# Weight conversion in a PSUM bank, wider spacing and a later pair of subtractions, in a fused attention and two-MLP kernel

## Chip, cores and metric

One core of one Trainium2 chip runs the whole program. The metric is device time in microseconds (us), the median over runs. The engines are PE (TensorE: matmuls, and PEld its weight loads), DVE (VectorE), ACT (ScalarE), POOL (GpSimd) and SP (SyncE, which here issues nearly all DMAs).

## What is computed

The reference, cut to what matters:

```
q, k: RMS-normalised per head (batch 4, 12 heads, 448 tokens, 64 wide), times gains
attn = softmax(q k^T / 8) ; x = attn @ v            # x: 1792 tokens x 768
h = x @ w_in (768x2048) ; g = h * sigmoid(h) ; x = g @ w_out (2048x768)
h = x @ w2_in (768x1024) ; s = h * softmax(h) ; n = layernorm(s) * g_ln
out = n @ w2_out (1024x768)
```

The eight input arrays are float64 in memory. The program itself turns the weights to fp32 while it runs: it reads each number as two 32-bit words and puts an fp32 together from them.

## The kernel before

**Stages.** Attention takes the first 250 us or so. Then comes the first MLP. Its 2048 hidden columns are cut into 8 groups g of 256, its tokens into 4 blocks b of 512, 512, 512 and 256. A step (g, b) has two halves: `mlp1_a` multiplies the tokens by the group's part of `w_in` into two PSUM banks `hp` (pool `ps_mm`, 2 banks; 18 matmuls each, since every operand is a high part and a low remainder, and three products of them are summed), and `mlp1_b` multiplies the result `gt` by `w_out` in six groups of six matmuls, d = 0 to 5, each into a bank `xps`. PE does `mlp1_a` of step i+1 ahead of `mlp1_b` of step i. The steps stand in the order (0,0), (0,1), ... (5,3), then (6,0), (6,1), (7,0), (7,1), (6,2), (7,2), (6,3), (7,3). The last stage is the second MLP. It works on pairs of 128-token tiles as 2x2 blocks, and needs only seven block products where eight would be usual, at the price of sums and differences of blocks.

**PSUM.** There are eight banks. In the first MLP two are `hp`, two belong to `P_["x"]` and four to `P_["y"]`. The six groups of a step take them in the order x y y x y y, so with four y banks each bank comes back one whole step later.

**Who empties them.** ACT reads `hp` twice (`gf`, L872, and `gt`, L873); POOL forms the low part of `gt` (L874). DVE adds every `xps` to its accumulator in SBUF (L897; L895 copies in the first group).

**Conversions.** `stages` is one conversion of 384 columns, by six steps: `load` (SP, a 384 KB DMA into `raw`), `mag` (ACT, L157, absolute value of the high words into `cva`), then on DVE `clamp` (L160), `shift` (L164), `sign` (L168) and `low` (L172), whose result is `cvt`. Then ACT rounds it (`hi`, L127) and POOL takes the remainder (`lo`, L130). From group 1 on the results go either straight to a `slab` in SBUF, or through the staging tile `stg` to DRAM (the `park` tensors, L133), from where `unpark` (L771) brings them back as slabs of 768 KB per half when they are due. For `w2_in` and `w2_out` differences of blocks (`sub`, L192) and a gain (L182) are added. The pools give two `raw`, two `cva`, four `cvt` and four `stg` buffers, so load k waits until `low` of conversion k-2 has read its `raw`.

**Order.** All queues are in the order in which the program emits. A clock in units near a microsecond advances with each group of matmuls (`MM`: 0.2105 for each 512-column matmul, 0.111 for each 256-column one), and `tick` emits each step of a conversion when its time in `STEP[ph]` after the conversion's start has come (load 0, mag 4.5, clamp 5.7, shift 6.3, sign 6.9, low 7.5). Starts of conversions are at least `EV` units apart. Each `xps` addition is emitted with its matmuls, ahead of the conversion steps that come due during them. The second MLP has a planner of its own (`timetable`) that orders by due times; `operands` gives it the chain of sums (`mix`), roundings (`hi`, ACT, L1007) and remainders (`lo`).

Of the kernel before, what the change touches and what calls it, by code (L numbers as in the profile page):

```python
# [11 lines left out]
F32 = mybir.dt.float32  # L12
F32R = mybir.dt.float32r
U32 = mybir.dt.uint32
AF = mybir.ActivationFunctionType
ALU = mybir.AluOpType
AX = mybir.AxisListType
PSUM = bass.MemoryType.PSUM
# [19 lines left out]
HW_MIN = float(np.array(0x38100000, np.uint32).view(np.float32))  # L38
HW_MAX = float(np.array(0x47EFFFFF, np.uint32).view(np.float32))
# [60 lines left out]
def fused_kernel(ctx: ExitStack, tc, nat, qt, gqk, w_in, w_out, w2_in, w2_out, g_ln, out):  # L100
    nc = tc.nc
# [7 lines left out]
    P_ = {}  # L109
# [5 lines left out]
    CB = {}  # L115
# [20 lines left out]
    def stages(src, c, ph, w, g=None, quad=None):  # L136

        n = 384
        k = {}

        def load():
            k["raw"] = P_["cv"].tile([128, n, 2], U32, name="raw", tag="raw", bufs=CB.get("raw"))
            nc.sync.dma_start(out=k["raw"][:, :, :].rearrange("p n t -> p (n t)"),
                              in_=src.bitcast(U32)[:, 2 * c * n:2 * (c + 1) * n])  # L150

        def mag():
            k["lw"], k["hw"] = k["raw"][:, :, 0], k["raw"][:, :, 1]
            a = k["a"] = P_["cv"].tile([128, n], U32, name="cva", tag="cva", bufs=CB.get("cva"))[:, :]
            t = k["t"] = a if ph == 0 else P_["cv"].tile([128, n], U32, name="cvt", tag="cvt", bufs=CB.get("cvt"))[:, :]
            k["af"], k["tf"] = a.bitcast(F32), t.bitcast(F32)
            nc.scalar.activation(out=k["af"], in_=k["hw"].bitcast(F32), func=AF.Abs)  # L157

        def clamp():
            nc.vector.tensor_scalar(out=k["af"], in0=k["af"], scalar1=HW_MIN, scalar2=HW_MAX,  # L160
                                    op0=ALU.max, op1=ALU.min)

        def shift():
            nc.vector.tensor_scalar(out=k["a"], in0=k["a"], scalar1=3, scalar2=0x3FFFFFFF,  # L164
                                    op0=ALU.logical_shift_left, op1=ALU.bitwise_and)

        def sign():
            nc.vector.scalar_tensor_tensor(out=k["t"], in0=k["hw"], scalar=0xC0000000, in1=k["a"],  # L168
                                           op0=ALU.bitwise_and, op1=ALU.bitwise_or)

        def low():
            nc.vector.scalar_tensor_tensor(out=k["t"], in0=k["lw"], scalar=29, in1=k["t"],  # L172
                                           op0=ALU.logical_shift_right, op1=ALU.bitwise_or)
        base = list(zip(STEP[ph], (load, mag, clamp, shift, sign, low)))
        if quad is None:
            return base + list(zip(STEP[ph][6:], halves(lambda: k["tf"], w, CL[ph])))

        name, q = quad

        def gain():  # L180
            if g is not None:
                nc.scalar.activation(out=k["tf"], in_=k["tf"], func=AF.Identity, scale=g)  # L182
            q[name] = k["tf"]

        def sub(o, a, b):

            def f():
                if o == "T1":
                    q[o] = P_["cv"].tile([128, n], F32, name="cvt", tag="cvt", bufs=CB.get("cvt"))[:, :]
                else:  # L190
                    q[o] = q[{"T2": "T1", "T3": "12", "T4": "T2"}[o]]
                nc.vector.tensor_tensor(out=q[o], in0=q[a], in1=q[b], op=ALU.subtract)  # L192
            return f

        def out(x, t):
            return list(zip((t, t + .9, t + 2.9), halves(lambda: q[x], w[x], "p")))
        base.append((8.7, gain))
        if name == "11":
            base += out("11", 9.9)
        elif name == "12":  # L200
            base += [(9.5, sub("T1", "12", "11"))] + out("T1", 10.5)
        elif name == "22":
            base += [(9.5, sub("T3", "22", "12"))] + out("22", 9.3) + out("T3", 11.0) + \
                [(12.0, sub("T2", "22", "T1"))] + out("T2", 12.8)
        else:
            base += out("21", 10.4) + [(11.3, sub("T4", "21", "T2"))] + out("T4", 12.2)
        return base
# [607 lines left out]
    psy = ExitStack()  # L815

    def after_attention():

        late.close()
        P_["x"] = psx.enter_context(tc.tile_pool(name="ps_x", bufs=2, space=PSUM, side="right", reuse_waits="tile"))  # L820
        acc1 = ctx.enter_context(tc.tile_pool(name="acc1", bufs=1))
        x2.append(acc1.tile([128, 2, KD, 256], F32, name="x2_0"))
        acc2 = mlp1.enter_context(tc.tile_pool(name="acc2", bufs=1, reuse_waits="tile"))
        x2.extend([acc2.tile([128, KD, CW[b]], F32, name=f"x2_{b}") for b in range(1, NC)])
        P_["big2"] = mlp1.enter_context(tc.tile_pool(name="big2", bufs=2, reuse_waits="tile"))
        P_["y"] = psy.enter_context(tc.tile_pool(name="ps_y", bufs=4, space=PSUM, reuse_waits="tile"))

    HL = [(0, 1), (1, 0), (0, 0)]

# [15 lines left out]
    def fetch(g, every=6.8):  # L845
        pool = P_["big2"] if g % 2 else big
        enqueue(pool, ws[g], w_in[g], every)
        enqueue(pool, ws[g], w_out[g], every)
# [134 lines left out]
    def op(k, e, took, f, after=(), tiles=(), lat=.15):  # L983
        plan2[k] = [e, took, lat, list(after), list(tiles), None]
        run2[k] = f

    def tens(e, o, a, b, f):
        e.tensor_tensor(out=o, in0=a, in1=b, op=f)  # L988

    def operands(l, p, tile, first, e):  # L990

        r, w = raws[l].setdefault(p, {}), (3, 4)[l]

        def mix(n, e=e):
            def f():
                o, a, b = MIX[l][n]
                if n == "S1":
                    r[n] = raws[l]["S1"]
                tens(en[e], r[o], r[a], r[b], ALU.add if n == "S1" else ALU.subtract)
                r[n] = r[o]  # L1000
            return f

        def hi(n):
            def f():
                k = slots[l].pop(0)
                t = parts[l, p, n] = (k, home[l](k))
                nc.scalar.copy(out=t[1][:, 0], in_=r[n])  # L1007
            return f

        def lo(n):  # L1010
            def f():
                t = parts[l, p, n][1]
                tens((nc.gpsimd, nc.vector)[l], t[:, 1], r[n], t[:, 0].bitcast(F32), ALU.subtract)
            return f
        TM = (1.0 if l == 0 else 1.3) if e == "p" else (.5, .69)[l]
        S1 = ("m%d" % l, p)
        E = {"p": "POOL", "v": "DVE"}[e]

        def key(x, n):
            return (x, l, p, n)  # L1020
        op(key("mix", "S1"), E, TM, mix("S1"), first["21"] + first["22"], [S1] + tile("21") + tile("22"))
        op(key("mix", "S2"), *((E, TM) if l == 0 else ("DVE", .75)), mix("S2", "v" if l else e), first["11"] + [key("mix", "S1"), key("lo", "S1")], [S1] + tile("11"))
        op(key("mix", "S3"), E, TM, mix("S3"), first["11"] + [key("mix", "S1")] + [key("lo", "S1")] * l,
           tile("11") + tile("21"))
        op(key("mix", "S4"), E, TM, mix("S4"), [key("mix", "S2"), key("lo", "12")] + first["12"], [S1] + tile("12"))
        prev = [("hi", l, p - 1, ORDER[l][-1])] if p else []
        for n in ORDER[l]:
            src = {"S1": [S1], "S2": [S1], "S3": tile("21"), "S4": tile("12")}.get(n) or tile(n)
            aft = first[n] if n in first else [key("mix", n)]
            if (l, p, n) == (1, 0, "S1"):  # L1030
                aft = aft + [("add", 0, 1, i) for i in (1, 2, 5)]
            op(key("hi", n), "ACT", (.47, .6)[l], hi(n), aft + prev, src + [("r%d" % l, p, n)])
            op(key("lo", n), ("POOL", "DVE")[l], (1.0, .69)[l], lo(n), [key("hi", n)], src + [("r%d" % l, p, n)])
            prev = [key("hi", n)]
# [192 lines left out]

    steps = [(g, b) for g in range(NMG - 2) for b in range(NC)]
    steps += [(6, 0), (6, 1), (7, 0), (7, 1), (6, 2), (7, 2), (6, 3), (7, 3)]
    EV = 3.7  # L1230

    def spare(x):
        if x < 2:
            enqueue(None, [], parked[x], EV, park=parks[x])
        elif x < 6:
            enqueue4(w2_in, EV, park2[0], x - 2, None)
        else:
            enqueue4(w2_out, EV, park2[1], x - 6, gln4)

    def ahead(g):  # L1240
        if g < NMG - 2:
            fetch(g + 1, EV)
        for x in ((0, ), (1, 2), (3, ), (4, 5), (6, ), (7, 8), (9, ))[g]:
# [143 lines left out]
```

## Time and profile before

| | |
|---|---|
| median of 3 runs | 958.27 us (956.87 to 961.7) |
| the profiled execution | 959.88 us, of which the span from first to last instruction is 958.1 us |
| PE busy | 937.7 us, 98% |
| DVE, POOL, ACT busy | 766.2, 540.1 and 514.6 us |

The page gives busy time by engine, slices of the span, the chain that ended last and the costliest groups of instructions. The trace behind it answers with the instructions of one line or one engine in a stretch, with what ended the idle time before each. "L866 <-ACT gt L873" reads: the instruction of line 866 had to wait, and what ended its wait was the ACT instruction of line 873.

### The profile page before, as it was taken

How to read it: one execution, taken by the hardware profiler on the slowest of the kernel's cores; microseconds unless marked ns; L12 is line 12 of the kernel's file. 1: busy time of each engine (PE TensorE's matmuls, PEld its weight loads, DVE VectorE, ACT ScalarE, POOL GpSimd, SP SyncE). 2: the span in 40 equal slices, each digit the busy share in tenths (PEclk: the TensorE clock that was granted, in tenths of full speed). 3: DMA queues.
4: the chain of work that ended last, by engine and by line, in shares of the span. 5: the costliest groups of instructions: out<-in, count | busy, mean ns of one | idle time of the engine just before them, and what ended most of it. 6: DMA issues, size and time to landing. Idle time of an engine off the chain costs nothing. (4 is left out here: it accounts for less than half of the span.)

```text
span 958.1 us, 15217 instructions
## 1 busy us (share of the span) xinstructions
PE 937.7 (98%) x4981; PEld 774.1 (81%) x4981; DVE 766.2 (80%) x1450; ACT 514.6 (54%) x1215; POOL 540.1 (56%) x679
## 2 busy tenths in 40 slices
PE   8999999999999999999999999899999999999998
PEld 7776676776778888888888888778889889889997
DVE  6999999999648879899889999866223878887885
ACT  6898999999733333344334453443022445455553
POOL 7888889898534354554646455445142445557530
PEclk9999999999999999999999999999999999999999
DMA  6776767775413444555456464686378611111101
GB/s 195 197 222 166 208 193 201 197 201 139 127 34 100 128 121 135 187 157 155 156 165 218 131 184 119 206 299 235 140 301 340 254 34 50 58 59 39 60 1 66
DMA packets 73502, 147.89 MB, mean 154 GB/s; under 512 B 10256, under 2 KB 48912, under 8 KB 73168
## 3 DMA queue, kind: packets, MB, share of 16 engines
q1 hardware_dynamic: 73136, 146.93, 49.4%
q8 instruction: 39, 0.64, 0.3%
q14 instruction: 39, 0.32, 0.1%
q10 hardware_dynamic: 288, 0.01, 0.0%
HBM read 90.44 MB, written 34.60 MB: 131 GB/s over the span
## 5 line engine op out<-in xcount | busy, mean ns | idle before, releaser
L866 PE MATMUL hp<-xt,slab 128*128 128x512 f32 (+1 forms) x1152 | 241.5, 367 | 5.8 <-ACT gt L873 5.8
L889 PE MATMUL xps<-gt,slab 128*128 128x512 f32 (+1 forms) x1152 | 235.6, 363 | 0.0
L866 PEld LDWEIGHTS hp<-xt,slab 128*128 128x128 f32 x1152 | 198.6, 190 | 42.1 <-ACT gt L873 7.3
L889 PEld LDWEIGHTS xps<-gt,slab 128*128 128x128 f32 x1152 | 197.1, 189 | 33.8
L874 POOL TENSOR_TENSOR gt<-gf,gt 128x512 fp32r<-128x512 f32 (+1 forms) x64 | 80.9, 1264 | 117.0 <-ACT gt L873 91.9
L897 DVE TENSOR_TENSOR x<-xps,x 128x512 f32<-128x512 f32 (+1 forms) x168 | 101.4, 615 | 50.8 <-PE xps L889 50.8
L157 ACT ACTIVATE cva<-raw 128x384 f32<-128x384 f32 x96 | 53.5, 560 | 149.3 <-DMA raw<-w_out 78.0
L484 DVE TENSOR_SCALAR_CACHE_REDUCE sp<-sp,ms 128x448 f32<-128x448 f32 x168 | 109.3, 684 | 9.3 <-PE sp L476 7.8
L130 POOL TENSOR_TENSOR stg<-cvt,stg 128x384 fp32r<-128x384 f32 x64 | 72.3, 1136 | 69.3 <-ACT stg L127 69.3
L520 POOL TENSOR_SCALAR p<-p,st 128x448 f32<-128x448 f32 x144 | 97.9, 691 | 18.9 <-DVE st L511 14.0
L495 ACT ACTIVATE p<-sp,st 128x448 f32<-128x448 f32 x144 | 96.7, 686 | 7.8 <-DVE sp L484 7.4
L1056 PE MATMUL y<-slab,gt 128*128 128x384 f32 x504 | 91.7, 341 | 2.3 <-DVE gt L988 2.3
L1056 PE MATMUL x<-slab,xr 128*128 128x512 f32 x378 | 91.9, 395 | 0.0
L1056 PEld LDWEIGHTS y<-slab,gt 128*128 128x128 f32 x504 | 88.6, 191 | 3.3 <-DVE gt L988 2.6
L130 POOL TENSOR_TENSOR slab<-cvt,slab 128x384 fp32r<-128x384 f32 x48 | 54.5, 1137 | 61.3 <-ACT slab L127 61.3
L1056 PEld LDWEIGHTS x<-slab,xr 128*128 128x128 f32 x378 | 69.5, 188 | 14.0 <-ACT gt L1067 0.2
L528 PE MATMUL tp<-ident,p 128*128 128x128 f32 x504 | 77.5, 274 | 1.1 <-ACT ht L557 0.9
L168 DVE SCALAR_TENSOR_TENSOR cvt<-raw,cva 128x384 uint32<-128x384 uint32 x88 | 73.3, 833 | 5.5
L172 DVE SCALAR_TENSOR_TENSOR cvt<-raw,cvt 128x384 uint32<-128x384 uint32 x88 | 72.3, 821 | 2.3
L160 DVE TENSOR_SCALAR cva<-cva 128x384 f32<-128x384 f32 x96 | 43.9, 458 | 34.0 <-ACT cva L157 33.9
L528 PEld LDWEIGHTS tp<-ident,p 128*128 128x128 f32 x504 | 60.8, 140 | 11.3 <-ACT ht L557 2.7
L476 PE MATMUL sp<-Z 128*128 128x448 f32 x138 | 64.3, 466 | 2.5 <-ACT y L318 1.4
(163 smaller groups left out, 1605.5 us busy)
## 6 DMA issues: line engine op xcount, KB each, us to landing
Z<-X SPq DMA_DIRECT2D x92, 224.0 KB, 3.6
raw<-w_in SPq DMA_DIRECT2D x48, 384.0 KB, 3.4
raw<-w_out SPq DMA_DIRECT2D x48, 384.0 KB, 3.2
park<-stg SPq DMA_DIRECT2D x32, 384.0 KB, 4.1
slab<-park SPq DMA_DIRECT2D x16, 768.0 KB, 8.9
nat<-nat SPq DMA_DIRECT2D x23, 480.0 KB, 4.1
vn<-nat SPq DMA_DIRECT2D x24, 256.0 KB, 3.9
park0T<-stg SPq DMA_DIRECT2D x16, 384.0 KB, 4.2
```

The lines of the kernel that those rows point to most:

```text
L130: en[e].tensor_tensor(out=k["o"][1], in0=f(), in1=k["o"][0].bitcast(F32), op=ALU.subtract)
L168: nc.vector.scalar_tensor_tensor(out=k["t"], in0=k["hw"], scalar=0xC0000000, in1=k["a"], op0=ALU.bitwise_and, op1=ALU.bitwise_or)
L172: nc.vector.scalar_tensor_tensor(out=k["t"], in0=k["lw"], scalar=29, in1=k["t"], op0=ALU.logical_shift_right, op1=ALU.bitwise_or)
L484: nc.vector.tensor_scalar(out=sp, in0=sp, scalar1=c["ms"][:, g:g + 1], scalar2=None, op0=ALU.mult, op1=ALU.min, accum_out=c["st"][:, 0, i: ...
L495: nc.scalar.activation(out=P(i), in_=c["sp"][i][:, :], func=AF.Exp, bias=c["st"][:, 0, i:i + 1], scale=-1.0, accum_out=c["st"][:, 1, i:i + 1])
L520: nc.gpsimd.tensor_scalar(out=p, in0=p, scalar1=r, scalar2=0.0, op0=ALU.mult, op1=ALU.add)
L528: nc.tensor.transpose(tp[:, o + t * 128:o + (t + 1) * 128], p[:, a:a + 128], ident[:, :])
L866: nc.tensor.matmul(hp[0][:, 0:CW[b]], ws[g][0][:, pw, kd * 256 + m * 128:kd * 256 + (m + 1) * 128], xT[(b, kd)][:, px, :], start=(i == 0), ...
L874: nc.gpsimd.tensor_tensor(out=gt[0][:, 1, m, :], in0=gf[:, :], in1=gt[0][:, 0, m, :].bitcast(F32), op=ALU.subtract)
L889: nc.tensor.matmul(xps[:, 0:CW[b]], ws[g][1][:, pw, m * 768 + d * 128:m * 768 + (d + 1) * 128], gt[0][:, px, m, :], start=(j == 0), stop=( ...
L897: nc.vector.tensor_tensor(out=o, in0=xp, in1=o, op=ALU.add)
L1056: nc.tensor.matmul(ps(b), s_[:, px, k, :], W[l, PAIR[x]][:, pw, k * n:(k + 1) * n], start=(not k0 and j == 0), stop=(j == 3 * w - 1), skip ...
```

## The change

```diff
         def mag():
             k["lw"], k["hw"] = k["raw"][:, :, 0], k["raw"][:, :, 1]
-            a = k["a"] = P_["cv"].tile([128, n], U32, name="cva", tag="cva", bufs=CB.get("cva"))[:, :]
-            t = k["t"] = a if ph == 0 else P_["cv"].tile([128, n], U32, name="cvt", tag="cvt", bufs=CB.get("cvt"))[:, :]
-            k["af"], k["tf"] = a.bitcast(F32), t.bitcast(F32)
-            nc.scalar.activation(out=k["af"], in_=k["hw"].bitcast(F32), func=AF.Abs)
+            k["a"] = P_["cv"].tile([128, n], U32, name="cva", tag="cva", bufs=CB.get("cva"))[:, :]
+            nc.scalar.activation(out=k["a"].bitcast(F32), in_=k["hw"].bitcast(F32), func=AF.Abs)
 
         def clamp():
-            nc.vector.tensor_scalar(out=k["af"], in0=k["af"], scalar1=HW_MIN, scalar2=HW_MAX,
+            k["p"] = k["a"] if ph == 0 else P_["cp"].tile([128, 512], U32, name="cp", tag="cp")[:, 0:n]
+            nc.vector.tensor_scalar(out=k["p"].bitcast(F32), in0=k["a"].bitcast(F32), scalar1=HW_MIN, scalar2=HW_MAX,
                                     op0=ALU.max, op1=ALU.min)
 
         def shift():
-            nc.vector.tensor_scalar(out=k["a"], in0=k["a"], scalar1=3, scalar2=0x3FFFFFFF,
+            nc.vector.tensor_scalar(out=k["p"], in0=k["p"], scalar1=3, scalar2=0x3FFFFFFF,
                                     op0=ALU.logical_shift_left, op1=ALU.bitwise_and)
 
         def sign():
-            nc.vector.scalar_tensor_tensor(out=k["t"], in0=k["hw"], scalar=0xC0000000, in1=k["a"],
+            nc.vector.scalar_tensor_tensor(out=k["p"], in0=k["hw"], scalar=0xC0000000, in1=k["p"],
                                            op0=ALU.bitwise_and, op1=ALU.bitwise_or)
 
         def low():
-            nc.vector.scalar_tensor_tensor(out=k["t"], in0=k["lw"], scalar=29, in1=k["t"],
+            t = k["a"] if ph == 0 else P_["cv"].tile([128, n], U32, name="cvt", tag="cvt", bufs=CB.get("cvt"))[:, :]
+            k["tf"] = t.bitcast(F32)
+            nc.vector.scalar_tensor_tensor(out=t, in0=k["lw"], scalar=29, in1=k["p"],
                                            op0=ALU.logical_shift_right, op1=ALU.bitwise_or)
...
-        P_["y"] = psy.enter_context(tc.tile_pool(name="ps_y", bufs=4, space=PSUM, reuse_waits="tile"))
+        P_["cp"] = psy.enter_context(tc.tile_pool(name="ps_c", bufs=1, space=PSUM, reuse_waits="tile"))
+        P_["y"] = psy.enter_context(tc.tile_pool(name="ps_y", bufs=3, space=PSUM, reuse_waits="tile"))
...
-        op(key("mix", "S3"), E, TM, mix("S3"), first["11"] + [key("mix", "S1")] + [key("lo", "S1")] * l,
+        op(key("mix", "S3"), E, TM, mix("S3"), first["11"] + [key("mix", "S1")] + [key("lo", "S2" if e == "v" else "S1")] * l,
            tile("11") + tile("21"))
-        op(key("mix", "S4"), E, TM, mix("S4"), [key("mix", "S2"), key("lo", "12")] + first["12"], [S1] + tile("12"))
+        op(key("mix", "S4"), E, TM, mix("S4"), [key("lo", "S2")] * (l and e == "v") + [key("mix", "S2"), key("lo", "12")] + first["12"], [S1] + tile("12"))
...
-    EV = 3.7
+    EV = 4.0
```

The intermediate results of `clamp`, `shift` and `sign` go to one PSUM bank `cp`, and `low` reads it and writes `cvt` in SBUF. The accumulators lose that bank: three y banks. Conversions from group 1 on start at least 4.0 units apart. In the second product of the second MLP, where DVE forms the sums (`e == "v"`: the first and the last pair), `mix S3` and `mix S4` come after `lo S2`. The matmuls keep their order: PE's sequence is the same before and after.

DVE, the start of the conversions of group 1 (clamp, shift, sign, low of one conversion, an accumulator copy among them), before:

```order
L160 TENSOR_SCALAR cva<-cva 128x384
L164 TENSOR_SCALAR cva<-cva 128x384
L895 COPY x_0_3919<-xps 128x2x256
L168 SCALAR_TENSOR_TENSOR cvt<-raw,cva 128x384
L172 SCALAR_TENSOR_TENSOR cvt<-raw,cvt 128x384
```

and of the change:

```order
L159 TENSOR_SCALAR cp<-cva 128x384
L163 TENSOR_SCALAR cp<-cp 128x384
L897 COPY x_0_3919<-xps 128x2x256
L167 SCALAR_TENSOR_TENSOR cp<-raw,cp 128x384
L173 SCALAR_TENSOR_TENSOR cvt<-raw,cp 128x384
```

As many instructions as before stand there; what has changed is where they read and write (line numbers rise by up to 2).

SP, around the two `unpark` of the last group's weights (`park_3681` and `park_3682`, at the start of steps (6,0) and (6,1)); `raw` loads are conversions, `park1T` and the others are stores of finished ones. Before:

```order
L149 DMA raw<-w_out 128x768 x8
L133 DMA park_3690<-stg 256x1x384
L149 DMA raw<-w_out 128x768
L133 DMA park1T_3693<-stg 256x1x384
L149 DMA raw<-w_out 128x768
L133 DMA park_3695<-stg 256x1x384
L771 DMA slab<-park_3681 128x1536 x2
L133 DMA park1T_3696<-stg 256x1x384
```

and of the change:

```order
L149 DMA raw<-w_in 128x768
L149 DMA raw<-w_out 128x768 x4
L772 DMA slab<-park_3681 128x1536 x2
L149 DMA raw<-w_out 128x768 x3
L772 DMA slab<-park_3682 128x1536 x2
L149 DMA raw<-w_out 128x768
L133 DMA park_3690<-stg 256x1x384
```

The conversions have moved back against the steps: ten loads of `w_out` stood ahead of the first `unpark`, now four do, and the stores that stood around the two now come behind both.

DVE, the second product of the first pair (`gf<-gf,e` is mix S2, `e<-e` mix S3, `e<-e,gf` mix S4; `gt<-gf,gt` is a remainder `lo` of S1 or S2, `gt<-e,gt` of S4 and S3), before:

```order
L988 TENSOR_TENSOR gt<-gf,gt 128x512
L988 TENSOR_TENSOR gf<-gf,e 128x512
L988 TENSOR_TENSOR e<-e 128x512
L988 TENSOR_TENSOR e<-e,gf 128x512
L988 TENSOR_TENSOR gt<-gf,gt 128x512
L988 TENSOR_TENSOR gt<-e,gt 128x512 x2
```

and of the change:

```order
L990 TENSOR_TENSOR gt<-gf,gt 128x512
L990 TENSOR_TENSOR gf<-gf,e 128x512
L990 TENSOR_TENSOR gt<-gf,gt 128x512
L990 TENSOR_TENSOR e<-e,gf 128x512
L990 TENSOR_TENSOR e<-e 128x512
L990 TENSOR_TENSOR gt<-e,gt 128x512 x2
```

`lo S2` is now ahead of both differences, and S4's stands ahead of S3's.

## Rows read from the trace of the kernel before

**Rows 1.** The page, busy us of PE (share of the span) and its instructions.

```profile
PE 937.7 (98%) x4981; PEld 774.1 (81%) x4981; DVE 766.2 (80%) x1450; ACT 514.6 (54%) x1215; POOL 540.1 (56%) x679
```

**Rows 2.** Waits of PE, whole span: us in total, times, longest us.

```profile
PE hp L866 <- ACT gt L873: 5.8, 3, 3.7
PE y L1056 <- DVE gt L988: 2.3, 1, 2.3
```

**Rows 3.** Windows: us; busy PE, PEld, DVE, ACT, POOL; granted clock, DMA share, GB/s.

```profile
610.00:630.00 20.00, 15.63 (x73) 12.91 (x72) 13.32 (x23) 8.65 (x17) 8.90 (x9) 0.83 0.82 290
630.00:650.00 20.00, 18.53 (x82) 15.03 (x81) 16.11 (x28) 9.28 (x19) 10.09 (x10) 1.00 0.83 276
770.00:790.00 20.00, 17.67 (x82) 15.92 (x81) 14.10 (x25) 9.34 (x22) 9.82 (x11) 0.91 0.11 35
```

**Rows 4.** Timeline of PE, 600 to 740: start us, us, instructions [idle before].

```profile
604.14 8.32 PE L866 MATMUL hp<-xt,slab 128*128 128x512 f32 x36
612.30 4.47 PE L889 MATMUL xps<-gt,slab 128*128 128x256 f32 x36
620.42 6.92 PE L866 MATMUL hp<-xt,slab 128*128 128x512 f32 x18 [3.65 <-ACT gt L873]
...
650.36 8.32 PE L889 MATMUL xps<-gt,slab 128*128 128x512 f32 x36
```

**Rows 5.** Timeline of PE in the second MLP and at the end.

```profile
775.05 7.93 PE L1056 MATMUL y<-slab,gt 128*128 128x384 f32 x35 [2.33 <-DVE gt L988]
782.81 8.37 PE L1056 MATMUL x<-slab,xr 128*128 128x512 f32 x36
...
940.73 12.83 PE L1056 MATMUL x<-slab,gt 128*128 128x384 f32 x72
```

**Rows 6.** Line 149, the conversions' loads, 300 to 612 us, and who waited for them.

```profile
L149 SPq DMA_DIRECT2D raw<-w_in x40: 327/328/337, 313.5 to 573.6; - x40
L149 SPq DMA_DIRECT2D raw<-w_out x36: 327/328/336, 301.4 to 608.1; - x36
...
  ACT cva L157: 134.1, 73
...
DMA to landing us min/median/max: 2.9/3.2/4.4
```

**Rows 7.** Groups of DVE, 300 to 612 us: busy us, mean ns, idle before.

```profile
L172 DVE SCALAR_TENSOR_TENSOR cvt<-raw,cvt 128x384 uint32<-128x384 uint32 x76 | 64.4, 847 | 1.9
L168 DVE SCALAR_TENSOR_TENSOR cvt<-raw,cva 128x384 uint32<-128x384 uint32 x77 | 62.0, 805 | 5.0
...
L164 DVE TENSOR_SCALAR cva<-cva 128x384 uint32<-128x384 uint32 x76 | 43.0, 566 | 1.5
L160 DVE TENSOR_SCALAR cva<-cva 128x384 f32<-128x384 f32 x76 | 35.6, 468 | 15.2 <-ACT cva L157 15.0
```

**Rows 8.** Tile cva, 300 to 612 us: ns min/median/max of sign.

```profile
L168 DVE SCALAR_TENSOR_TENSOR cvt<-raw,cva x77: 541/559/1474, 300.2 to 611.6; 128x384 uint32<-128x384 uint32 x77
```

**Rows 9.** Groups of DVE, whole span, with operands in PSUM.

```profile
L988 DVE TENSOR_TENSOR x<-y,x 128x384 f32<-128x384 f32 x18 | 9.9, 549 | 4.5 <-PE y L1056 4.4
...
L988 DVE TENSOR_TENSOR y<-y,gt 128x512 f32<-128x512 f32 x3 | 2.1, 700 | 9.7 <-PE y L1056 9.7
```

**Rows 10.** Timeline of DVE: the last addition of step (5,2).

```profile
613.39 0.68 DVE L897 TENSOR_TENSOR x<-xps,x 128x512 f32<-128x512 f32 x1
```

**Rows 11.** Line 149, 612 to 648 us.

```profile
DMA to landing us min/median/max: 3.4/6.6/8.7
```

**Rows 12.** Timeline of ACT, 606 to 640 us.

```profile
625.11 0.51 ACT L127 CAST stg<-cvt 128x384 fp32r<-128x384 f32 x1 [4.73 <-DMA park1T<-stg]
```

**Rows 13.** Timeline of ACT, 766 to 778 us: the rounding of S2, first pair.

```profile
771.60 0.62 ACT L1007 CAST gt<-gf 128x512 fp32r<-128x512 f32 x1 [2.67 <-DVE gf L988]
```

**Rows 14.** Timeline of DVE, 766 to 778 us: mix S4 and lo S2, first pair.

```profile
772.91 1.48 DVE L988 TENSOR_TENSOR e<-e,gf 128x512 f32<-128x512 f32 x1
774.32 0.68 DVE L988 TENSOR_TENSOR gt<-gf,gt 128x512 fp32r<-128x512 f32 x1
```

## The prediction

> **What bounds the kernel now.** I read the busy table first: PE works 937.7 of 958.1 us [rows 1], so only time in which PE stands still or is slow can be won, and its own instructions do not change. Then the waits of PE: of 20 us idle, two groups lie where this change reaches. PE waits three times, 5.8 us in all, for ACT to empty an `hp` bank, and once, 2.3 us, for DVE in the second MLP [rows 2]. The windows give the granted clock around them: 0.83 of full speed between 610 and 630 us, 0.91 between 770 and 790, and 1.00 between 630 and 650 although PE also stood still there [rows 3]. So the waits of 3.65 us [rows 4] and 2.33 us [rows 5] were followed by a stretch at 1.2 GHz, and one of about 1.5 us (20 less the 18.53 us of PE work in the window 630 to 650) was not.
>
> What each place costs, clock included, is read from starts in PE's timeline. **First place:** a half step of 36 matmuls with 512 columns takes 612.30 - 604.14 = 8.16 us, one with 256 columns at most 4.47. From 612.30 to 650.36 lie one short and three long halves: 38.06 us where 4.4 + 3 x 8.16 = 28.9 would do. Lost: 9.2 us [rows 4]. **Second place:** 35 matmuls of 384 columns run from 775.05 to 782.81, 7.76 us; at the end of the program 72 of them take 12.83, so 35 take 6.24. Lost: 1.5 us of clock plus the wait of 2.33, 3.9 us [rows 5]. Together 13.1 us can be won, no more.
>
> **Why ACT is late at the first place.** The conversions' loads tell it. 76 loads went out between 301.4 and 608.1 us, one in 306.7 / 75 = 4.09 us, and ACT's `mag` waited for the landing of 73 of them, 134.1 us in all [rows 6]. A load waits for `low` of the conversion before last, `mag` for the load, `clamp` for `mag`: with two `raw` buffers this is a ring, two conversions long, of 8.2 us, and the ring sets the pace. The program asks for more while it has conversions queued: 3.7 units, where a unit is 8.16 us / (36 x 0.2105) = 1.077 us, so one in 3.98 us. DVE and ACT run their queues in order, so what stands behind a late `clamp` or `mag` is late as well. The last addition of step (5,2), whose matmuls ended when PE went on at 604.14, started at 613.39, over 9 us late [rows 4, 10]. ACT's `gf` stood behind steps that waited for DVE in the same way, and PE for `gf`.
>
> **The change, part by part.** *Four steps through PSUM.* 88 conversions have four DVE steps each, means 468, 566, 805 and 847 ns, sum 2.69 us [rows 7]. The same sign instruction took between 541 and 1474 ns [rows 8]: its work is 0.54, the rest is being held. With one operand in PSUM and 384 columns the nearest row has 549 ns; reading and writing PSUM with 512 columns, 700 ns, is a ceiling for ours [rows 9]. I take 0.55 for each, since shape and operands are nearest: 2.2 us, 0.49 less; the ceiling gives 2.8, 0.11 more. DVE saves 88 x 0.49 = 43 us, none of it directly on PE's path. What counts is the ring: 8.2 us less one conversion's 0.49 is 7.7, or 3.85 us for each conversion; with the ceiling 8.3, or 4.15.
>
> The Trainium skill (SBUF — State Buffer, Who interferes with whom) says that a DVE instruction with two SBUF inputs, or in a two-port mode, and a GpSimd instruction that reads SBUF exclude each other on a shared port, and that one with at most one SBUF input and no such mode does not contend. The spread of sign agrees; no row here shows a conversion step out of PSUM. By the page the steps run unheld and the second rival below loses its ground; without it they could be held as before, which is that rival. The same skill (VectorE: DVE Perf Modes, Why PSUM operands drop a tier) speaks against the change: fp32 steps with a PSUM operand lose the double rate. By it clamp and shift gain nothing, and all of the gain must come from sign and low, which is how the 0.55 for all four has it.
>
> *Spacing.* 4.0 units are 4.31 us. That is above both 3.85 and 4.15, so the ring no longer sets the pace, and lateness from one conversion is made up in the next. `mag` then finds its data: it stands 4.5 units, 4.8 us, behind its load, and a load lands in 3.2. The price: conversions end later, by 0.3 units for each that is queued. They end where DVE is free again, and the slabs they feed are read a step or more later. SP's loads are moved past the two `unpark`, and the stores of `w2_out` now come behind both. I cost this at nothing.
>
> *One bank less.* The second y bank of a step comes back for its sixth group: d = 5 takes the bank of d = 1. Between them lie three groups of 8.16 / 6 = 1.36 us, so an addition that takes 0.68 may start up to 3.4 us late; in a short step (4.4 / 6 = 0.73 us a group, 0.41 an addition) 1.8 us. An addition now waits for at most two conversion steps, 1.1 us, since its lateness no longer grows. I cost it at nothing, covered by that margin; if the cover goes, see the second rival.
>
> *The `unpark`.* Each brings 1.5 MB at once, and between 612 and 648 us loads landed after 6.6 us in the median and 8.7 at worst, against 3.2 [rows 6, 11]; ACT stood 4.73 us for a staging buffer whose store was caught in it [rows 12]. The slabs stay where they are, so some of this stays: with loads that land up to 5 us late, `mag` would be about 3 us late, once or twice, behind which `gf` has the other half step as slack. I take 1.0 us left of 9.2; bounds 0 and 9.2.
>
> *First pair.* S2 is rounded at 771.60 + 0.62 = 772.2. `lo S2` then ends at 772.9 instead of 775.0 [rows 13, 14], and PE, free at 775.05 - 2.33 = 772.7, starts S2 almost at once. Next is S4, whose remainder stands behind both differences. Each took about 1.48 us beside POOL; an undisturbed addition of that size 0.69. So lo S4 ends between 772.9 + 2 x 0.69 + 0.69 = 775.0 and 772.9 + 2 x 1.48 + 0.68 = 776.5, while product S2 (12 of 72 matmuls in 12.83 us: 2.1) ends at 775.0: a wait of 0 to 1.5 us, below those that cost clock. I take one held and one free: 0.9 plus 0.2. Left: 1.1 of 3.9 us. At the last pair PE had no wait, and S4 has two products' time of slack; nothing there.
>
> **Sum.** -9.2 + 1.0 - 3.9 + 1.1 = -11.0 us. Against the profiled execution, 959.9, that is 948.9; it stood 1.6 us above the median, and from the median it is 947.3. I predict **948 us**.
>
> **Rivals.**
> 1. *The wait at the `unpark` stays.* The conversions now last longer into the stretch in which slabs come in, so DMA traffic instead of DVE holds `mag`, and PE waits again between 612 and 660 us. For it: the late landings [rows 11] and the 4.73 us [rows 12]. Against: 73 waits for data long before any slab was fetched [rows 6], and no stores of conversions between the two `unpark` any more. If all stays, only the first pair gives: 959.9 or 958.3 - 2.8, about 956; if half stays, 951.
> 2. *Three banks turn lateness into waits; slower.* Place: group d = 5 of the steps of groups 3 to 5. If the steps in PSUM are held or slow, so that additions stay as late as now, PE must wait for its bank until they are at most 3.4 us late: 9.2 - 3.4 = 5.8 us, in two or three waits of about 2 us, each with 1.5 us of clock behind it as at the second place, 4.5 us. The first place's 9.2 stay, the first pair gives 2.8: +7.5, 966 us. It decides at 3.4 us of lateness (1.8 in short steps), which needs a ring above 4.31 us, that is over 0.77 us for each PSUM step. Against: the 700 ns that a wider instruction takes [rows 9].
> 3. *The pair's edit only moves the wait* from S2 to S4: with 3.9 us not won and the rest as forecast, 951.
>
> **How the numbers follow.** Forecast 0.68, first rival 0.17, second 0.10, third 0.05. A measurement of this kernel tells about 0.5%, 4.8 us, from no change. The forecast (945 to 952) and the third rival are faster; of the first, 0.05 faster and 0.12 the same; the second is slower. Faster 0.78, same 0.12, slower 0.10. The range goes from everything won, 958.3 - 13.1 = 945.2, less the half microsecond by which runs differ, to the first rival in full: 944.5 to 956.5.
>
> **What would show it.** Right: the conversion steps near 550 ns with hardly any spread; ACT's wait for loads far below 134 us; additions starting within 1.5 us of their matmuls; no wait of PE above 2 us and a clock of 1.0 from 610 to 660 us; at the first pair a wait near 1 us, before S4. Wrong: waits of `xps` matmuls (L891) for DVE's additions (L899), which the kernel before does not have; PSUM steps above 0.77 us; a wait for `gt` again between 612 and 660 us behind a late load.

## The result and the profile after

The changed kernel takes 946.65 us in the median of 4 runs (946.23 to 947.21), the kernel before beside it 957.57 us: 0.9878 of it, 95% interval 0.9848 to 0.9908. A second series, beside the last runs below, gave 947.23 us and 0.9887 [0.9864, 0.991]. The forecast was 948.0 (944.5 to 956.5).

The page of after, against [rows 1], and its mean granted clock:

```profile
PE 933.3 (99%) x4981; PEld 771.9 (82%) x4981; DVE 727.1 (77%) x1450; ACT 513.8 (54%) x1215; POOL 520.7 (55%) x679
core 0: 944.9 us, clock 1.000
```

PE does the same 4981 matmuls, in 4.4 us less busy time, at a mean clock of 1.000 of full speed where the kernel before had 0.994. DVE is busy 39 us less, POOL 19 us less, although POOL's instructions are as before. Waits of PE from 300 to 944 us (in total, times, longest), against [rows 2]:

```profile
PE y L1058 <- DVE gt L990: 0.6, 2, 0.3
```

That is all that is left; the three waits for `hp` are gone. Windows of after, against [rows 3] (us; busy PE, PEld, DVE, ACT, POOL; clock, DMA share, GB/s), and PE's timeline there, against [rows 4]:

```profile
610.00:630.00 20.00, 20.00 (x106) 17.27 (x105) 13.21 (x29) 9.43 (x19) 9.63 (x10) 1.00 0.64 218
630.00:650.00 20.00, 20.00 (x90) 16.56 (x89) 16.00 (x30) 9.15 (x18) 10.09 (x10) 1.00 0.89 298
```

```profile
611.62 4.48 PE L891 MATMUL xps<-gt,slab 128*128 128x256 f32 x36
615.93 8.35 PE L868 MATMUL hp<-xt,slab 128*128 128x512 f32 x36
624.12 8.32 PE L891 MATMUL xps<-gt,slab 128*128 128x512 f32 x36
632.28 8.32 PE L868 MATMUL hp<-xt,slab 128*128 128x512 f32 x36
640.44 8.32 PE L891 MATMUL xps<-gt,slab 128*128 128x512 f32 x36
```

One short and three long halves take 640.44 - 611.62 = 28.82 us; they took 38.06 before. All 9.2 us of the first place have come back. The same subtraction measures this stretch in the experiments below. At the first pair two short waits stand where one of 2.33 us stood [rows 5]:

```profile
762.79 2.51 PE L1058 MATMUL y<-slab,gt 128*128 128x384 f32 x12 [0.33 <-DVE gt L990]
765.58 4.26 PE L1058 MATMUL y<-slab,gt 128*128 128x384 f32 x23 [0.28 <-DVE gt L990]
```

The conversion's steps, tile `cp`, 300 to 700 us (ns min/median/max), against [rows 7, 8]:

```profile
L159 DVE TENSOR_SCALAR cp<-cva x85: 543/552/562, 299.5 to 665.3; 128x384 f32<-128x384 f32 x85
L163 DVE TENSOR_SCALAR cp<-cp x85: 550/566/567, 300.1 to 665.9; 128x384 uint32<-128x384 uint32 x85
L167 DVE SCALAR_TENSOR_TENSOR cp<-raw,cp x85: 549/562/565, 300.7 to 667.0; 128x384 uint32<-128x384 uint32 x85
L173 DVE SCALAR_TENSOR_TENSOR cvt<-raw,cp x85: 540/553/555, 301.7 to 667.6; 128x384 uint32<-128x384 uint32 x85
```

Every step is at its 0.55 us, with a spread of some 20 ns where sign alone went from 541 to 1474. And line 149 from 300 to 612 us, against [rows 6]:

```profile
L149 SPq DMA_DIRECT2D raw<-w_in x40: 327/328/559, 314.9 to 586.8; - x40
L149 SPq DMA_DIRECT2D raw<-w_out x33: 327/328/334, 302.4 to 610.1; - x33
...
  ACT cva L155: 106.7, 54
DMA to landing us min/median/max: 3.0/3.2/5.2
```

73 loads in 307.7 us are one in 4.27 us; the program asks for 4.31.

Most of this agrees with the forecast; two signs that did not come are named further down. It doesn't say which part of the change did it: the parts are the PSUM steps with the bank they cost (A), the spacing (B) and the first pair's edit (C).

### The profile page after: what moved, and what is told of

Its sections match the earlier page's. It is cut to its first block, busy times and chain, and to the rows that moved or that the text cites. A ratio compares the mean times of both kernels' runs of the same rounds, so it can differ in the third digit from the quotient of the medians.

```text
span 944.9 us, 15380 instructions
## 1 busy us (share of the span) xinstructions
PE 933.3 (99%) x4981; PEld 771.9 (82%) x4981; DVE 727.1 (77%) x1450; ACT 513.8 (54%) x1215; POOL 520.7 (55%) x679
## 4 chain that ended last, share of the span: by engine, by line
PE 86%; DVE 5%; ACT 4%; DMA 2%; POOL 1%; issue 1%; SPq 0%; DVEq 0%; POOLq 0%; ACTq 0%
PE hp L868 24%; PE xps L891 24%; PE x L1058 11%; PE y L1058 10%; PE sp L477 4%; PE pv L572 4%; PE tp L529 3%; DVE sp L485 2%; ACT p L496 1%; DMA nat<-nat 1%; PE y L1155 1%; PE pv L575 1%; ACT ht L558 1%; PE tp L398 1%; DVE ms L313 0%
## 5 line engine op out<-in xcount | busy, mean ns | idle before, releaser
L868 PE MATMUL hp<-xt,slab 128*128 128x512 f32 (+1 forms) x1152 | 238.1, 364 | 0.0
L899 DVE TENSOR_TENSOR x<-xps,x 128x512 f32<-128x512 f32 (+1 forms) x168 | 103.3, 619 | 71.8 <-PE xps L891 71.7
L876 POOL TENSOR_TENSOR gt<-gf,gt 128x512 fp32r<-128x512 f32 (+1 forms) x64 | 74.0, 1157 | 117.6 <-ACT gt L875 82.0
L130 POOL TENSOR_TENSOR stg<-cvt,stg 128x384 fp32r<-128x384 f32 x64 | 65.7, 1036 | 58.0 <-ACT stg L127 54.6
L130 POOL TENSOR_TENSOR slab<-cvt,slab 128x384 fp32r<-128x384 f32 x48 | 48.7, 1015 | 81.2 <-ACT slab L127 81.2
L159 DVE TENSOR_SCALAR cp<-cva 128x384 f32<-128x384 f32 x88 | 48.8, 554 | 28.6 <-ACT cva L155 27.7
L874 ACT ACTIVATE gf<-hp 128x512 f32<-128x512 f32 (+1 forms) x64 | 34.7, 542 | 64.6 <-PE hp L868 64.4
L477 PE MATMUL sp<-X,lz 128*128 128x448 f32 x168 | 63.3, 379 | 0.5 <-POOL lz L417 0.5
```

What stands on the lines that cost most here:

```text
L130: en[e].tensor_tensor(out=k["o"][1], in0=f(), in1=k["o"][0].bitcast(F32), op=ALU.subtract)
L477: nc.tensor.matmul(sp[:, :], a_, k_, start=(w == 0), stop=(w == len(mm) - 1))
L868: nc.tensor.matmul(hp[0][:, 0:CW[b]], ws[g][0][:, pw, kd * 256 + m * 128:kd * 256 + (m + 1) * 128], xT[(b, kd)][:, px, :], start=(i == 0), ...
L876: nc.gpsimd.tensor_tensor(out=gt[0][:, 1, m, :], in0=gf[:, :], in1=gt[0][:, 0, m, :].bitcast(F32), op=ALU.subtract)
L899: nc.vector.tensor_tensor(out=o, in0=xp, in1=o, op=ALU.add)
```

## The experiments

Each run was timed in five rounds beside the kernel before on the same chip; kernels from different chips are compared by their ratios.

| kernel | median us | ratio to before [95%] |
|---|---|---|
| C | 957.08 | 0.9985 [0.9974, 0.9996] |
| B | 950.63 | 0.9921 [0.9902, 0.9940] |
| A | 957.22 | 0.9993 [0.9981, 1.0005] |
| B + C | 948.73 | 0.9900 [0.9879, 0.9920] |
| A + B | 948.64 | 0.9898 [0.9877, 0.9919] |
| A + C | 955.33 | 0.9963 [0.9951, 0.9974] |
| A + B + C, again | 947.23 | 0.9887 [0.9864, 0.9910] |
| three y banks alone | 967.21 | 1.0097 [1.0081, 1.0113] |
| three y banks + B | 958.38 | 0.9998 [0.9980, 1.0017] |
| A + C, spacing 3.85 | 952.79 | 0.9940 [0.9918, 0.9961] |
| A + C, first slab later | 955.95 | 0.9977 [0.9964, 0.9990] |
| first slab later alone | 961.48 | 1.0028 [1.0012, 1.0043] |

### The first pair's edit alone (C)

```diff
-        op(key("mix", "S4"), E, TM, mix("S4"), [key("mix", "S2"), key("lo", "12")] + first["12"], [S1] + tile("12"))
+        op(key("mix", "S4"), E, TM, mix("S4"), [key("lo", "S2")] * (l and e == "v") + [key("mix", "S2"), key("lo", "12")] + first["12"], [S1] + tile("12"))
```

with the line of `mix S3` as in the change.

> The kernel before with the later subtractions of the first and last pair alone. The changed kernel's two waits at the first pair were 0.33 and 0.28 us where the kernel before lost 3.9 us, clock included. If that part is independent of the rest, this kernel gains 3.3 us: about 954.3, ratio 0.9966; the three waits for hp between 612 and 660 us (5.8 us) stay. Rival: the conversions end late and POOL is then still busy beside the first pair, so the differences are held, S4 waits 1 to 1.5 us, and the gain is 2 us or less.

957.08 us, 0.9985: 1.4 us gained, at most 2.5 by the interval. Waits of PE:

```profile
PE hp L866 <- ACT gt L873: 6.4, 3, 3.1
PE y L1056 <- DVE gt L988: 0.6, 2, 0.3
```

The wait itself goes as forecast, and so does the stretch at 1.2 GHz behind it; the first place stays (37.72 us from 611.45 to 649.17, against 38.06). By time the edit gives less than the 2.8 us that were put on it. The time is the rival's, its reason isn't: S4 waits 0.29 us, not 1 to 1.5.

### The spacing alone (B)

```diff
-    EV = 3.7
+    EV = 4.0
```

> The kernel before with EV = 4.0 alone, conversion steps in SBUF and four y banks. By the theory of the ring (two conversions in 8.2 us, 4.09 each, below the 4.31 now asked for) the lateness goes and PE's wait for hp with it: about 949, additions within 2 us of their matmuls. By the rival that DVE's own load decides (2.69 for the steps, 0.8 for a difference and 1.1 for additions make 4.5 us for each 4.31 in the stretches with differences), additions are still 3 to 6 us late from 500 us on and the gain is 0 to 5 us.

950.63 us, 0.9921. The first place is nearly free with SBUF steps and four y banks:

```profile
612.01 4.48 PE L889 MATMUL xps<-gt,slab 128*128 128x256 f32 x36
...
640.83 8.32 PE L889 MATMUL xps<-gt,slab 128*128 128x512 f32 x36
```

```profile
PE hp L866 <- ACT gt L873: 1.4, 1, 1.4
```

That one wait lies at 683.18 us, behind the first place; the stretch itself, from 612.01 to 640.83 us, takes 28.82 us as in the changed kernel. The pair's wait of 2.3 us stays. By the starts and ends in the two engines' timelines the additions of step (5,3) come at most 2 us after their matmuls, as the theory of the ring has it, and those of step (7,0), where the wait lies, 10 to 12 us. One number in the program carries some 7.5 us of the change's 11.

### The PSUM steps and their bank, at the old spacing (A)

```diff
-            nc.vector.tensor_scalar(out=k["af"], in0=k["af"], scalar1=HW_MIN, scalar2=HW_MAX,
+            k["p"] = k["a"] if ph == 0 else P_["cp"].tile([128, 512], U32, name="cp", tag="cp")[:, 0:n]
+            nc.vector.tensor_scalar(out=k["p"].bitcast(F32), in0=k["a"].bitcast(F32), scalar1=HW_MIN, scalar2=HW_MAX,
...
-        P_["y"] = psy.enter_context(tc.tile_pool(name="ps_y", bufs=4, space=PSUM, reuse_waits="tile"))
+        P_["cp"] = psy.enter_context(tc.tile_pool(name="ps_c", bufs=1, space=PSUM, reuse_waits="tile"))
+        P_["y"] = psy.enter_context(tc.tile_pool(name="ps_y", bufs=3, space=PSUM, reuse_waits="tile"))
```

and the other three steps as in the change.

> The conversion steps in the PSUM bank and three y banks, EV = 3.7, the pair as before. By the theory that held steps make DVE late, this alone brings the first place's 9.2 us: about 949, steps at 0.55 us, additions at most 2 us late, no wait of xps matmuls for additions. By the theory of spacing, the program asks for one conversion in 3.98 us, lateness grows to more than 3.4 us in the stretches with differences, and PE waits at the sixth group of a step, 2 to 6 us in all: 951 to 955.

957.22 us, 0.9993: nothing, less than either theory had, although DVE was busy 730.1 us instead of 766. PE's waits for `hp` are gone, and one for a bank has come, 5.50 us at 621.41, in the sixth group of the short step (5,3). DVE there:

```profile
619.20 0.56 DVE L159 TENSOR_SCALAR cp<-cva 128x384 f32<-128x384 f32 x1 [6.75 <-ACT cva L155]
619.67 0.41 DVE L899 TENSOR_TENSOR x<-xps,x 128x256 f32<-128x256 f32 x1
```

DVE isn't busy: it stands 6.75 us in front of a `clamp`, and the step's additions stand behind it. `mag` comes late on ACT because two transfers are late: the rounding ahead of it stands 4.86 us for a staging buffer whose store is under way, and `mag` itself 0.74 us more for its load. The run of A + C below shows that row by row.

### The bank alone

```diff
-        P_["y"] = psy.enter_context(tc.tile_pool(name="ps_y", bufs=4, space=PSUM, reuse_waits="tile"))
+        P_["y"] = psy.enter_context(tc.tile_pool(name="ps_y", bufs=3, space=PSUM, reuse_waits="tile"))
```

> The kernel before with three y banks in place of four, conversion steps in SBUF, EV = 3.7 (the eighth bank stays empty). This prices the bank by itself. With additions 4 to 9 us late as before, the sixth group of a step must wait once lateness passes 3.4 us: 5.8 us of waits and about 4.5 us of lost clock on top of the time before, near 968, with PE waiting for L897. Rival: PE's waits only move from hp to the y bank, because both wait for the same late DVE, and the time stays within 2 us of the kernel before.

967.21 us, 1.0097, 9.3 us slower. PE's 5.8 us of waits for `hp` are gone, and in their place stands the wait that the prediction's second rival named:

```profile
PE xps L889 <- DVE x L897: 14.0, 5, 7.1
```

So A is two things that cancel at the old spacing: the bank costs 9.3 us, and the steps in PSUM, which are all that A has beyond this kernel, give them back.

### Spacing and first pair, no PSUM steps (B + C)

> The kernel before with the wider spacing (EV 4.0) and the later differences of the first pair; the four steps stay in SBUF and y keeps four banks. Theory that the spacing is what empties the first place: the spacing alone gave 950.6 and left the first pair's wait of 2.3 us with its clock stretch; with that gone it comes to 946.5 to 949.5, that is to the whole change's 946.65, and the PSUM steps are worth nothing in time here. Theory that the PSUM steps carry something of their own once the spacing is wide: 950 or more, with a wait for hp of over 1 us between 660 and 690 us.

948.73 us, 0.9900, and this wait:

```profile
PE hp L866 <- ACT gt L873: 1.8, 1, 1.8
```

It lies at 683.26 us, behind additions that came up to 11.6 us late at step (7,0), which four banks still cover. With A instead there was no such wait, and the ratio was 0.9878 and 0.9887 in the two series. So the time is that of the first theory, with the wait of the second. The difference of 1.2 to 2.1 us is of the size of the wait, and within the intervals. DVE spends 764.0 us here and 727.3 in the changed kernel's second series: A takes 37 us from an engine and at most about 2 from the time. What it does take is lateness: at step (7,0) of the changed kernel the additions come at most 4.9 us late.

The steps that stay in SBUF are the faster ones when nothing holds them (tile `cva` of this kernel, 300 to 700 us):

```profile
L164 DVE TENSOR_SCALAR cva<-cva x85: 344/361/1220, 300.0 to 672.3; 128x384 uint32<-128x384 uint32 x85
...
L160 DVE TENSOR_SCALAR cva<-cva x84: 342/360/1190, 303.6 to 671.4; 128x384 f32<-128x384 f32 x84
```

### PSUM steps and spacing, no pair's edit (A + B)

> The whole change without the later differences of the first pair. If the parts add: the changed kernel's 946.65 + 1.5 to 3.9 = 948.2 to 950.5, with a wait of about 2.3 us for the first pair near 765 us and one clock stretch of 3.4 us at the lower level, and nothing else. If the pair edit is worth nothing beyond its own wait: 946.7 to 948.

948.64 us, 0.9898. The pair's wait of 2.3 us is back, one of 0.7 us for a bank beside it. C on top of this gives 1.1 to 1.9 us by the two series' ratios; on B it gave 2.0, on A 2.9, alone 1.4. With intervals of about 1 to 3 us on each side these don't differ.

### The change at the old spacing (A + C)

> The whole change at the old spacing (EV 3.7). Theory that the burst of stores and loads at 610 to 620 us meets the short step (5,3) whenever the conversions stand at 3.7: a wait of y for an addition of about 5.5 us near 621 us with a halved clock after it, as with the PSUM steps alone (957.2), less the first pair: 953 to 956.5. Theory that the PSUM steps carry the gain of the first place (as the prediction had it): 947 to 949.

955.33 us, 0.9963. PE at the first place, and SP's issues with the time from issue to landing of the two raw loads at 609.85 and 612.81:

```profile
612.45 3.75 PE L891 MATMUL xps<-gt,slab 128*128 128x256 f32 x30
621.70 1.65 PE L891 MATMUL xps<-gt,slab 128*128 128x256 f32 x6 [5.51 <-DVE x L899]
623.15 9.94 PE L868 MATMUL hp<-xt,slab 128*128 128x512 f32 x36
632.92 8.55 PE L891 MATMUL xps<-gt,slab 128*128 128x512 f32 x36
```

```profile
607.65 1.16 SPq L772 DMA_DIRECT2D slab<-park  x2
608.85 0.52 SPq L133 DMA_DIRECT2D park1T<-stg  x1
609.85 0.34 SPq L149 DMA_DIRECT2D raw<-w_out  x1
610.24 1.46 SPq L133 DMA_DIRECT2D park1T<-stg  x1
611.80 0.59 SPq L133 DMA_DIRECT2D park<-stg  x1
612.81 0.53 SPq L149 DMA_DIRECT2D raw<-w_out  x1
```

```profile
DMA to landing us min/median/max: 8.9/9.0/9.0
```

ACT in between:

```profile
618.03 0.51 ACT L127 CAST stg<-cvt 128x384 fp32r<-128x384 f32 x1 [5.08 <-DMA park1T<-stg]
618.92 0.55 ACT L155 ACTIVATE cva<-raw 128x384 f32<-128x384 f32 x1 [0.38 <-DMA raw<-w_out]
620.36 0.58 ACT L875 ACTIVATE gt<-hp 128x512 fp32r<-128x512 f32 x1
```

Two slab halves and stores are under way, and two transfers are late among them. ACT can't round an earlier conversion before a store has freed a staging buffer, and stands 5.08 us for it; `mag`, next in its queue, then waits 0.38 us more for its raw load, which took 9 us where 3.2 is usual. Either of the two alone would have made `mag` late; no run has more staging buffers. Behind `mag` the `clamp` comes late, DVE's queue stands, PE waits for a bank, and the granted clock is 0.50 from about 619.7 to 626.5 us. From 612.45 to 641.32 lie one short and two long halves, 28.87 us, for which the changed kernel needs 632.28 - 611.62 = 20.66. Lost: 8.2 us. The whole old spacing costs as much: 955.33 - 947.23 = 8.1, with 959.0 and 958.9 for the kernel before on the two chips.

That the late queue costs PE so much here also needs the missing bank. Without the wait for it PE would have come to the second `hp` bank at 612.45 + 4.31 + 4.08 = 620.84, and ACT has emptied that bank at 620.36 + 0.58 = 620.94. So with four y banks the burst would have cost about 0.1 us at this place: an estimate from these rows, which no run can show, since `cp` takes the eighth bank.

In the changed kernel SP's order is another:

```profile
603.82 0.33 SPq L149 DMA_DIRECT2D raw<-w_out  x1
604.20 0.90 SPq L772 DMA_DIRECT2D slab<-park  x2
606.74 9.45 SPq L149 DMA_DIRECT2D raw<-w_out  x3
616.24 0.90 SPq L772 DMA_DIRECT2D slab<-park  x2
618.94 0.33 SPq L149 DMA_DIRECT2D raw<-w_out  x1
619.37 0.52 SPq L133 DMA_DIRECT2D park<-stg  x1
```

```profile
DMA to landing us min/median/max: 3.1/4.0/6.2
```

The last line is that of its raw loads from 603 to 630 us. No store falls between the slabs. From 600 to 620 us one store is issued here; seven are in A + C.

### Three banks with the wider spacing

The edits of the bank and of B together; the steps stay in SBUF.

> The kernel before with three y banks and the wider spacing; the steps stay in SBUF, the first pair as before. With the spacing alone the additions still came up to 5.5 us late at (4,1) and 6 to 12 us late at (6,1) and (7,0). Theory that the PSUM steps are what pays for the bank: waits of y for additions of 2 to 6 us at one to three of these places, 953 to 962. Theory that the spacing alone takes the lateness away and the bank is free: 949.5 to 951.5, as with four banks.

958.38 us, 0.9998. Against B alone (0.9921) the bank costs 0.77% or 7.4 us at this spacing too, in five waits for additions, the longest, 3.84, at 671.23:

```profile
PE xps L889 <- DVE x L897: 6.3, 5, 3.8
```

A + B, which is this kernel with the steps in PSUM, takes 948.64. So the PSUM steps are worth 9.7 us to a kernel with three banks, and that pays for the bank, with little over.

### The first slab one step later

```diff
-        if g == NMG - 2 and b < 2:
-            flow.append((0, lambda b=b: unpark(P_["big2"], ws[NMG - 1], parks[b])))
+        if g == NMG - 2 and b == 1:
+            flow += [(0, lambda x=x: unpark(P_["big2"], ws[NMG - 1], parks[x])) for x in range(2)]
```

First with A + C at the spacing of 3.7:

> The whole change at the old spacing (EV 3.7), as in the run that gave 955.33, with the first of the two parked slabs (1.5 MB) loaded back one step later, together with the second, before (6,1) instead of before (6,0). Theory that this load, issued at 608 us in front of a raw load that then took 9.05 us, makes the wait of 5.5 us at (5,3): the wait at 621 us is gone, additions of (5,3) are at most 2.5 us late; both slabs now stand in front of the raw loads at 624 us, which may be 10 to 16 us late and give a wait of 0 to 4 us at (6,0) or (6,1): 946.7 to 952. Theory that at EV 3.7 the conversions are simply too dense for three banks, whatever is loaded: the wait at (5,3) stays at 3 us or more: 953 to 957.

955.95 us, 0.9977: the time of the second theory with the picture of the first. The wait at (5,3) shrinks from 5.51 to 1.25 us, and one of 4.55 us stands one step later, where the slabs now are:

```profile
616.89 0.98 PE L891 MATMUL xps<-gt,slab 128*128 128x256 f32 x6 [1.25 <-DVE x L899]
...
625.89 6.96 PE L891 MATMUL xps<-gt,slab 128*128 128x512 f32 x30
637.41 2.92 PE L891 MATMUL xps<-gt,slab 128*128 128x512 f32 x6 [4.55 <-DVE x L899]
```

The wait follows the slab. A later slab among the same stores wins nothing; a raw load issued behind the four halves took 10.7 us, and here it is the load alone that ACT waits for, 8.36 us in front of `mag`.

Then in the kernel before:

> The kernel before with that move of the first slab alone. Theory that the slab's load also starts the first place of the kernel before: its waits of PE for hp between 612 and 660 us and the stretches of halved clock shrink by half or more: 950 to 955. Theory that the held SBUF steps at EV 3.7 set the first place, as the prediction had it: waits and time as before, 956.5 to 960.

961.48 us, 1.0028, worse than either theory had it. PE, in one of its quicker executions (959.19 us):

```profile
618.87 8.48 PE L866 MATMUL hp<-xt,slab 128*128 128x512 f32 x36 [3.23 <-ACT gt L873]
...
644.81 5.80 PE L866 MATMUL hp<-xt,slab 128*128 128x512 f32 x18 [4.91 <-ACT gt L873]
```

The wait for `hp` at (5,3) stays, 3.23 after 3.65 us, with no slab under way (the first is issued at 627.20): there the late DVE queue of the held steps is enough. Behind the slabs stands a second one: ACT waits 7.77 us for a raw load in front of `mag`. In the kernel before, too, PE's two later waits at the first place, 0.71 and 1.47 us, stand behind waits of ACT for transfers, 4.73 us for a store [rows 12] and 4.19 for a load. So two causes are at work at the first place, the held steps and the burst, and moving the burst leaves the one and moves the other.

### The change at a spacing of 3.85, and again at 4.0

```diff
-    EV = 4.0
+    EV = 3.85
```

> The whole change with a spacing between the two, EV 3.85. If only the meeting of slab loads and raw loads decides: no wait over 1 us, 946.5 to 948.5, as at 4.0. If the room between conversions decides: something between 946.65 (EV 4.0) and 955.33 (EV 3.7), a wait for an addition of 1 to 4 us near 615 to 640 us, 949 to 953.

952.79 us, 0.9940: between the two, with three waits for additions of 0.31, 2.45 and 0.29 us. From 600 to 620 us three stores are issued. The longest stands in step (6,0), behind a wait of ACT of 5.12 us for a store. The theory of more room holds in time; the stores are among the slabs in part, so the other isn't excluded.

> The changed kernel again, on the chip of these runs: 945.5 to 948, 0.986 to 0.991 of the kernel before. Beside the spacing and the pair edit without the PSUM part (948.73, 0.9900), the PSUM part with its bank is worth 2 us if the wait of 1.8 us for hp that was left there is all of it.

947.23 us, 0.9887: as forecast, with one wait of 0.3 us for an addition and the clock at its upper level throughout.

## Why the prediction was right, and which of its steps were not

**Right, with its reasons:** the 13.1 us that could be won. The first place gave back all of its 9.2 us, the second its wait but for 0.6 us, and the clock of both: the profiled span went from 958.1 to 944.9, in the second series to 946.3. By the medians it was 10.9 and 11.7 us.

**Right:** a PSUM step of 0.55 us, taken from the row of 549 ns [rows 9]. No step is held any more, and POOL, on the other side, is busy 15 us less than in B + C (521.8 against 536.9). The Trainium skill (SBUF — State Buffer, Who interferes with whom) says that a DVE instruction with at most one SBUF input, outside the two-port modes, does not contend with GpSimd; the trace agrees. Clamp and shift take 552 and 566 ns with PSUM, where the free ones in SBUF take 360 and 361. The Trainium skill (VectorE: DVE Perf Modes, Why PSUM operands drop a tier) says that a PSUM operand leaves fp32 at the single rate; the trace agrees here too. The gain is in the holds alone: sign and low went from means of 805 and 847 ns [rows 7] to medians of 562 and 553, clamp from 468 up to 552, and shift stayed at 566.

**Wrong: "What counts is the ring".** The forecast had the shorter ring win the first place, with the spacing to let it. By its own figures the shorter ring wasn't needed: the old one, 4.09 us, was already below the 4.31 that the wider spacing asks for, and B, with the steps in SBUF, frees the first place. The ring did shorten: in A, 78 loads went out between 301.2 and 609.6 us, one in 4.01, near the 3.98 that the program asks at 3.7, and from the starts in DVE's timeline additions came at most 2 us after their matmuls until (5,2), where they came 9 us after them before. But A gave 0.9993. One late queue is enough for a wait there when a bank is missing, and the burst around the slabs made one by itself.

**Wrong: the order on SP "at nothing".** The stores now come behind both slabs, and I named that and priced it at zero. The three kernels at 3.7 with the steps in PSUM lose 8.2 to 8.8 us where slabs and stores meet, and all those at 4.0 nothing there, whatever their steps and banks. That the order does this, rather than the lower rate of conversions, fits the runs at 3.85 and with the later slab, but it is argued: no run kept 3.7 and moved the stores alone. B also has additions that are less late ahead of 600 us, 2.5 to 3.3 us at step (4,3) where the kernel before has 8.4 to 9.4, so the rate has a share. How much each has stays open.

**Right in the sum, not by itself: the bank "at nothing".** It holds only with PSUM steps and wide spacing together. Without the steps the bank cost 9.3 us at 3.7 and 7.4 at 4.0; without the spacing a wait of 5.5 us is left. The second rival's price (10.3 us without the first pair's 2.8) was near what the bank alone cost; its condition, additions late by over 3.4 us or 1.8 in short steps, is where the longer waits stand. Its limit on the PSUM steps, 0.77 us, was not the only way to such lateness: a late load does it with steps of 0.55.

**Two signs that did not come.** ACT's wait for loads was to fall far below 134 us, and is 106.7. In B it is 119.5 with the first place free, in A 123.0 with nothing won: it doesn't tell the kernels apart. Lateness is read from the additions. These were to start within 1.5 us of their matmuls; they do at the first place, but come up to 2.5 us late at (4,1) and (6,1) and 3.0 to 4.9 at (7,0), which three banks just cover here. In the second series they come 3.6 to 5.4 us late there, and PE waits 0.3 us.

**Mis-sized: the two small terms.** The first slab was to leave 1.0 us and left none. The first pair was to give 2.8 us; its wait went from 2.33 to 0.6 with the clock stretch, yet by time it gave 1.1 to 2.9 in four comparisons. The 1.5 us of clock in that term is not lost in every kernel. Behind the same wait of 2.33 us the 35 matmuls took 7.93 us in the kernel before [rows 5] and, at the upper level of the clock, 6.36 in A:

```profile
773.67 6.36 PE L1058 MATMUL y<-slab,gt 128*128 128x384 f32 x35 [2.33 <-DVE gt L990]
```

The two terms' errors cancel in part, and that the gain came by another carrier doesn't show in the sum: -11.0 forecast, -10.9 and -11.7 measured. That the sum fits so closely is luck in this. (The lower end of the range is 945.2 - 0.5 = 944.7 by its own terms, not 944.5.)

**The rivals.** The first, a wait at the slabs, is what the kernel would have had without the wider spacing (955.33, near its 956). The third did not come: 0.33 us before S2 and 0.28 before S4.

## What to carry to other kernels

When two causes make one engine late at one place, price each with the other still there: the steps in PSUM with their bank won nothing (957.22), moving the slab won nothing (961.48), and the wider spacing, after which neither shows there, won 7 us. An engine's busy time saved (37 us of DVE) is worth what it pays for, here a PSUM bank. When a spacing is changed, read the order of every DMA queue behind it: which loads and stores fall beside a large transfer may be worth more than the pace itself, and moving the large transfer among the same stores only moves the wait.

## What the hardware did that I had not expected

A 384 KB raw load behind two slab halves and a few stores took 9 us and behind four halves 10.7, where 3.2 is usual.

The length of PE's wait alone doesn't tell what the clock does after it. The granted clock was at 1.2 GHz for 6.8 us at the waits of 5.5 us (A, A + C) and 3.65 us (the kernel before), and for 3.4 us at those of 4.91 us (the first slab later alone), 2.45 us (spacing 3.85) and 2.33 us (the kernel before, B, A + B). It stayed at 2.4 GHz after 1.78 us (B + C), but also after 3.23 us (the first slab later alone) and after the same 2.33 us in A and in the kernel with three y banks alone.

The SBUF steps `clamp` and `shift` had a floor of 342 ns and a ceiling of 1220 in the same form: the steady 0.55 us out of PSUM is slower than the free case, and still made fewer additions late.
